# A rebuilt decode-attention-plus-MLP backward kernel: 32x32 vector transposes, tiled TensorE matmuls, weights in slices

## Chip, cores and metric

The kernel runs on one core of one Trainium2 chip. The metric is the device time of one launch in microseconds (us). TensorE is PE in the profile (its weight loads PEld), VectorE is DVE, ScalarE is ACT, GpSimd is POOL and SyncE is SP.

## What is computed

One decode step of two branches that share a layer norm, with all gradients. Inputs and outputs are bf16.

```python
B, Sq, D = 2, 1, 576;  Hq, Hkv, Sk, Dh = 32, 16, 4096, 128;  F = 4608
xn = layernorm(x)
q = (xn @ wq), 32 heads;  k, v = caches [2, 16, 4096, 128], each used by 2 query heads
p = softmax(q k^T * Dh**-0.5);  o = p v;  attn = o @ wo
mlp = ((xn @ w_gate) * (xn @ w_up)) @ w_down
out = x + attn + mlp
returns out and the gradients of x, k_cache, v_cache, wq, wo, w_gate, w_up, w_down for grad_out
```

The caches are 33.5 MB each and their gradients are as large; the five weights are 4.7 to 5.3 MB each, and so are their gradients. The gradients of the caches are outer products: dV[key, :] is the sum over two query heads of p[key] times dO, and dK[key, :] is the sum of dS[key] times q.

## The kernel before

Work comes in three stages, in the order of the code, and a scheduler orders each engine's instructions within what the tile pools allow.

- **Preamble** (lines 111 to 193). Layer norm; wq and wo are loaded whole; wo is transposed on PE (line 173); q and dO for all heads come out transposed, with two columns per weight load.
- **Eight head groups** (loop at lines 233 and 234: 2 batches, 4 groups of G = 4 key-value heads). For each group SP loads four K and four V heads of 1 MB (lines 266 and 272; pools of five buffers each). `scores_pass` (line 217) turns each head by PE: 32 transposes of 128x128 (line 208), eight copies out of PSUM (DVE line 213, ACT line 211) and eight score matmuls of 512 columns (line 225), whose output rows are 8 used rows out of 128, copied to SBUF (line 230). Softmax on rows of 4096 (lines 282 to 292); P and dS are transposed on PE (`rows_T`, line 300) and contracted with V and K, two moving columns per 128x128 weight load (lines 311 and 358). `outer_grad` (line 318) makes dV and dK: 32 matmuls of 512 columns each over 98 rows (line 326), one PSUM bank each, copied to bf16 on ACT for dV (line 336), on ACT and DVE in turn for dK (lines 336 and 334), and stored from POOL in pieces of 256 KB (line 339).
- **Tail** (line 369 on). wo and wq are loaded a second time, then the three MLP weights, each whole; each is transposed on PE where needed (lines 427 and 438); then the five weight gradients are made, copied out and stored in pieces of 64 to 144 KB (lines 559 to 587).

Of the kernel before, what the change touches and what calls it, by code (L numbers as in the profile page):

```python
# [8 lines left out]
AF = mybir.ActivationFunctionType  # L9
ALU = mybir.AluOpType  # L10
# [3 lines left out]
P = 128  # L14


@with_exitstack
def kernel(
# [41 lines left out]
    EPS = 1e-5  # L60

    nfull = D // P
    rem = D - nfull * P
    ND = nfull + (1 if rem else 0)
    DOFF = [c * P for c in range(nfull)] + ([D - P] if rem else [])
    DLO = [0] * nfull + ([P - rem] if rem else [])

    const = ctx.enter_context(tc.tile_pool(name="const", bufs=1))
    ps = ctx.enter_context(tc.tile_pool(name="ps", bufs=2, space=bass.MemoryType.PSUM))

    def ps_tr(shape, dtype=BF16):
# [12 lines left out]

    evac_state = [0]

    def evac(out_ap, in_ap, scale=None, engine=None):
        if engine is None:
            engine = "v" if (evac_state[0] % 2 == 0) else "s"
            evac_state[0] += 1  # L90
        if engine == "v":
            if scale is None:
                nc.vector.tensor_copy(out=out_ap, in_=in_ap)  # L93
            else:
                nc.vector.tensor_scalar(out_ap, in_ap, float(scale), None, op0=ALU.mult)
# [6 lines left out]
    ev_state = [0]

    def ev(out_ap, in_ap):
        if ev_state[0] % 2 == 0:
            nc.vector.tensor_copy(out=out_ap, in_=in_ap)
        else:
            nc.scalar.copy(out_ap, in_ap)
        ev_state[0] += 1

    ident = const.tile([P, P], BF16, name="ident")
    make_identity(nc, ident[:])

    x_bf = const.tile([2, D], BF16, name="x_bf")
    nc.sync.dma_start(x_bf[:], A_x.rearrange("b s d -> (b s) d"))
    x_f = const.tile([2, D], FP32, name="x_f")
    nc.vector.tensor_copy(x_f[:], x_bf[:])
    dy_bf = const.tile([2, D], BF16, name="dy_bf")
    nc.sync.dma_start(dy_bf[:], grad_out.rearrange("b s d -> (b s) d"))
    dy_f = const.tile([2, D], FP32, name="dy_f")  # L120
    nc.vector.tensor_copy(dy_f[:], dy_bf[:])
# [4 lines left out]
    xc = const.tile([2, D], FP32, name="xc")  # L126
    nc.vector.tensor_scalar(xc[:], x_f[:], mu[:], None, op0=ALU.subtract)
    xsq = const.tile([2, D], FP32, name="xsq")
    var = const.tile([2, 1], FP32, name="var")
    nc.vector.tensor_tensor_reduce(  # L130
        out=xsq[:], in0=xc[:], in1=xc[:], scale=1.0 / D, scalar=0.0,
# [7 lines left out]
    xn_f = const.tile([2, D], FP32, name="xn_f")  # L139
    nc.vector.tensor_scalar(xn_f[:], xc[:], rstd[:], None, op0=ALU.mult)  # L140
# [3 lines left out]
    def rows_to_T(rows_bf, name):  # L144
        tp = ps_tr([P, ND, 2], BF16)
        for c in range(ND):
            nc.tensor.transpose(tp[:, c, :], rows_bf[0:2, DOFF[c]:DOFF[c] + P], ident[0:2, 0:2])
        t = const.tile([P, ND, 2], BF16, name=name)
        nc.vector.tensor_copy(t[:], tp[:])
        return t  # L150

    xnT = rows_to_T(xn_bf, "xnT")
    dyT = rows_to_T(dy_bf, "dyT")

    qT_all = const.tile([P, Hq, 2], BF16, name="qT_all")
    doT_all = const.tile([P, Hq, 2], BF16, name="doT_all")
    oT_all = const.tile([P, Hq, 2], BF16, name="oT_all")
    dqT_all = const.tile([P, Hq, 2], BF16, name="dqT_all")

    with tc.tile_pool(name="w1", bufs=1) as w1:  # L160
        wq_sb = w1.tile([P, ND, HD], BF16, name="wq_sb")
        if nfull > 0:
            nc.sync.dma_start(wq_sb[:, 0:nfull, :], A_wq[0:nfull * P, :].rearrange("(c p) n -> p c n", p=P))
        if rem:
            nc.sync.dma_start(wq_sb[:, nfull, :], A_wq[D - P:D, :])
        wo_nat0 = w1.tile([P, Hq, D], BF16, name="wo_nat0")
        nc.sync.dma_start(wo_nat0[:], A_wo.rearrange("(c p) n -> p c n", p=P))
        woT_sb = w1.tile([P, ND, HD], BF16, name="woT_sb")
        for c in range(ND):
            for h8 in range(0, Hq, 8):  # L170
                tp = ps_tr([P, 8, P], BF16)
                for i in range(8):
                    nc.tensor.transpose(tp[:, i, :], wo_nat0[:, h8 + i, DOFF[c]:DOFF[c] + P], ident[:, :])
                ev(woT_sb[:, c, h8 * Dh:(h8 + 8) * Dh], tp[:].rearrange("p i d -> p (i d)"))

        qT_ps = ps_acc([P, Hq, 2])
        for h in range(Hq):
            for c in range(ND):
                lo = DLO[c]
                nc.tensor.matmul(  # L180
                    qT_ps[:, h, :], lhsT=wq_sb[lo:P, c, h * Dh:(h + 1) * Dh],
                    rhs=xnT[lo:P, c, :], start=(c == 0), stop=(c == ND - 1),
                )
        nc.vector.tensor_copy(qT_all[:], qT_ps[:])
        doT_ps = ps_acc([P, Hq, 2])
        for h in range(Hq):
            for c in range(ND):
                lo = DLO[c]
                nc.tensor.matmul(
                    doT_ps[:, h, :], lhsT=woT_sb[lo:P, c, h * Dh:(h + 1) * Dh],  # L190
                    rhs=dyT[lo:P, c, :], start=(c == 0), stop=(c == ND - 1),
                )
        nc.scalar.copy(doT_all[:], doT_ps[:])

    okview = out_2.rearrange("b h (p c) d -> b h p c d", p=P)
    ovview = out_3.rearrange("b h (p c) d -> b h p c d", p=P)
    kview = A_k_cache.rearrange("b h (p c) d -> b h p c d", p=P)
    vview = A_v_cache.rearrange("b h (p c) d -> b h p c d", p=P)

    with tc.tile_pool(name="grp", bufs=1) as gp:  # L200
        GR = 32 * (G - 1) + 2
        tt_state = [0]

        def transposed_tile(src_sb, kt, tagname):
# [417 lines left out]
```

## Time and profile before

| | us |
|---|---|
| median of 2 runs (lowest, highest) | 1140.95 (1140.0, 1141.89) |
| span of the profiled execution | 1133.8 |
| PE, DVE, ACT, POOL busy in it | 861.0, 504.6, 517.7, 287.3 |

The profile comes from one execution, whose own device time is not given apart; its span is taken here, and the median of the runs lies 7.2 us above it. No engine is busy for the whole span, so the average says little: each stage is read for itself.

### The profile page before, as it was taken

The page shows a single profiled execution, that of the slowest core. Times are in us where ns is not written, and L with a number is a line of the kernel's source. Part 1 is how long each engine was busy: PE and PEld are TensorE (multiplying, and loading weights), DVE is VectorE, ACT ScalarE, POOL GpSimd, SP SyncE. Part 2 cuts the span into 40 slices and gives each one's busy share as a digit, 9 for nine tenths or more (in the row PEclk, how much of TensorE's full clock was granted, in tenths as well). Part 3 has the DMA queues.
Part 4 walks back from the last instruction along what each step waited for, and adds up shares of the span by engine and source line. Part 5 has one row for each costly group of instructions (what it writes and reads, how often), then busy time and mean ns, then how long its engine had stood idle before and what let it go on. Part 6 is the DMA issues. An engine that isn't in the chain of part 4 may idle for free. (4 is left out here: it accounts for less than half of the span.)

```text
span 1133.8 us, 20144 instructions
## 1 busy us (share of the span) xinstructions
PE 861.0 (76%) x8208; PEld 511.8 (45%) x8208; DVE 504.6 (45%) x870; ACT 517.7 (46%) x900; POOL 287.3 (25%) x615
## 2 busy tenths in 40 slices
PE   3877788878768877878877878885599497786764
PEld 3755445535445544545553544551279463231210
DVE  1246155346436526615615635533141134774443
ACT  0346556556556555655645646662151230223332
POOL 0100221221131122123023023023000001677775
PEclk9878579678688888867858969975695689656555
DMA  9170760671581483185077057034990500444443
GB/s 345 49 331 3 289 266 39 221 300 74 186 334 76 149 318 128 47 323 226 1 270 288 38 189 294 38 124 190 376 334 26 209 1 33 155 153 141 153 142 123
DMA packets 54429, 197.94 MB, mean 175 GB/s; under 512 B 8472, under 2 KB 21280, under 8 KB 43584
## 3 DMA queue, kind: packets, MB, share of 16 engines
q1 hardware_dynamic: 24768, 104.15, 24.4%
q0 software_dynamic: 29568, 92.50, 21.6%
q8 instruction: 64, 1.05, 0.4%
q14 instruction: 29, 0.24, 0.1%
HBM read 104.14 MB, written 92.48 MB: 173 GB/s over the span
## 5 line engine op out<-in xcount | busy, mean ns | idle before, releaser
L336 ACT CAST dVst<-ps_dkv 128x512 bf16<-128x512 f32 x256 | 142.2, 586 | 120.4 <-PE ps_dkv L326 76.6
L326 PE MATMUL ps_dkv<-doBD,p_sb 98*128 98x512 bf16 x256 | 128.4, 524 | 49.1 <-ACT dVst L336 46.7
L326 PE MATMUL ps_dkv<-qsBD,ds_sb 98*128 98x512 bf16 x256 | 105.5, 462 | 51.0 <-ACT dKst L336 26.8
L334 DVE CAST dKst<-ps_dkv 128x512 bf16<-128x512 f32 x128 | 88.3, 690 | 110.8 <-PE ps_dkv L326 73.7
L339 POOL DMA_DIRECT2D out_dram<-dVst x128 | 68.3, 541 | 259.8 <-ACT dVst L336 259.8
L208 PE MATMUL ps_tr<-ident,V 128*128 128x128 bf16 x1024 | 98.0, 234 | 38.7 <-DVE vT L213 28.0
L208 PEld LDWEIGHTS <-K 128*128 128x128 bf16 x1024 | 83.0, 107 | 79.1 <-issue 43.8
L208 PEld LDWEIGHTS <-V 128*128 128x128 bf16 x1024 | 80.1, 106 | 80.3 <-issue 62.0
L336 ACT CAST dKst<-ps_dkv 128x512 bf16<-128x512 f32 x128 | 75.0, 586 | 86.9 <-PE ps_dkv L326 51.3
L208 PE MATMUL ps_tr<-ident,K 128*128 128x128 bf16 x1024 | 104.9, 237 | 7.3 <-DMA K<-in_A_k_cache_dram 6.0
L339 POOL DMA_DIRECT2D out_dram<-dKst x128 | 68.3, 539 | 148.2 <-ACT dKst L336 70.0
L225 PE MATMUL ps_sc<-kT,qM 128*128 128x512 bf16 x256 | 93.8, 412 | 2.2 <-DVE kT L213 1.0
L213 DVE COPY vT<-ps_tr 128x512 bf16<-128x512 bf16 x171 | 68.1, 422 | 59.9 <-PE ps_sc L225 42.3
L582 PE MATMUL ps_g<-rows,xnP 128*128 128x512 bf16 x130 | 64.5, 565 | 36.7 <-DVE gwq_st L93 11.4
L213 DVE COPY kT<-ps_tr 128x512 bf16<-128x512 bf16 x171 | 68.4, 420 | 48.6 <-PE ps_sc L225 27.5
L225 PE MATMUL ps_sc<-vT,doM 128*128 128x512 bf16 x256 | 89.4, 413 | 0.0
L211 ACT COPY kT<-ps_tr 128x512 bf16<-128x512 bf16 x85 | 50.0, 588 | 37.5 <-PE ps_sc L225 9.7
L211 ACT COPY vT<-ps_tr 128x512 bf16<-128x512 bf16 x85 | 49.7, 585 | 33.0 <-PE ps_sc L225 12.1
L326 PEld LDWEIGHTS <-ds_sb 98*128 98x128 bf16 x256 | 27.7, 109 | 75.2 <-issue 69.0
L568 POOL DMA_DIRECT2D out_dram<-gwo_st x32 | 17.2, 539 | 171.5 <-ACT gwo_st L98 164.7
L300 PEld LDWEIGHTS <-ds_sb 128*128 128x128 bf16 x256 | 31.5, 144 | 58.0 <-issue 57.5
L301 DVE COPY dsT<-ps_tr 128x64 bf16<-128x64 bf16 x32 | 6.1, 192 | 106.0 <-PE ps_tr L300 106.0
(175 smaller groups left out, 1382.7 us busy)
## 6 DMA issues: line engine op xcount, KB each, us to landing
K<-in_A_k_cache_dram SPq DMA_DIRECT2D x32, 1024.0 KB, 9.8
V<-in_A_v_cache_dram SPq DMA_DIRECT2D x32, 1024.0 KB, 6.8
out_dram<-dVst POOLq DMA_DIRECT2D x128, 256.0 KB, 8.0
out_dram<-dKst POOLq DMA_DIRECT2D x128, 256.0 KB, 3.5
wd_sb<-in_B_w_down_dram SPq DMA_DIRECT2D x1, 5184.0 KB
out_dram<-gwd_st POOLq DMA_DIRECT2D x36, 144.0 KB, 2.1
wo_nat<-in_A_wo_dram SPq DMA_DIRECT2D x1, 4608.0 KB, 28.5
wo_sb<-in_A_wo_dram SPq DMA_DIRECT2D x1, 4608.0 KB
```

Source lines behind the costliest of these rows:

```text
L208: nc.tensor.transpose(tp[:, i, :], src_sb[:, c, :], ident[:, :])
L211: nc.scalar.copy(t[:], tp[:])
L213: nc.vector.tensor_copy(t[:], tp[:])
L225: nc.tensor.matmul(s_ps[:], lhsT=masks[l][:].rearrange("p l r -> p (l r)"), rhs=tiles[kt][l][:].rearrange("p c k -> p (c k)"), start=(l == ...
L300: nc.tensor.transpose(tp[:, i, :], src[:, c * P:(c + 1) * P], ident[:, :])
L301: nc.vector.tensor_copy(t[:, 8 * c8:8 * c8 + 8, :].rearrange("p c (l r) -> p c l r", l=G), tp[:, :, :].rearrange("p c (l r) -> p c l r", l ...
L326: nc.tensor.matmul(pk[:, :], lhsT=rows_src[0:GR, c * P:(c + 1) * P], rhs=rhsBD[0:GR, :, :].rearrange("p l d -> p (l d)"), start=True, stop ...
L334: nc.vector.tensor_copy(st[:, :, i, :], pk[:, :].rearrange("p (l d) -> p l d", l=G))
L336: nc.scalar.copy(st[:, :, i, :], pk[:, :].rearrange("p (l d) -> p l d", l=G))
L339: nc.gpsimd.dma_start(oview[b, hkv][:, 8 * c8:8 * c8 + 8, :], st[:, l, :, :])
L568: nc.gpsimd.dma_start(out_ap[j * P:(j + 1) * P, :], st[:])
L582: nc.tensor.matmul(pk[:], lhsT=xnP[:, DOFF[c]:DOFF[c] + P], rhs=rows[:, t * 512:(t + 1) * 512], start=True, stop=True)
```

## The change

The kernel is written anew around one idea: no PE transposes of K and V. A head of K (128 partitions by 4096 bf16) is read as 128x2048 four-byte elements, each a pair of neighbouring bf16, and DVE transposes it in blocks of 32x32 (`t32`). A partition then holds pairs of features, and the score matmul picks the even or the odd one with a moving operand of step two; its weights `W` are block-diagonal and built by POOL (lines 382 and 386), so that all 128 output rows are used: 4 blocks of keys by 8 query heads. A head still takes eight score matmuls of 512 columns, but their result is 128x1024, not 128x4096 (line 414). P and dS are turned by `t32` as well (lines 490 and 511). `contract` has 32 weight columns (rows of P) and 128 moving columns (V or K as loaded), written to four blocks of 32 output partitions in turn; `outer` has 32 rows, in pairs into two PSUM banks, so that one copy takes 1024 columns; one store is 1 MB. The heads of both batches in a group are done one after another (g outside, b inside). Between attentions stands one ninth of the MLP, forward and backward (`mlp_slice`), and wq and wo are loaded by group and once. `evac` gives each copy to DVE or ACT by a running sum. Loads share ten 8 KB buffers ("nat"), stores three ("st"), transposed data two ("X").

```diff
+    def evac(out, in_, cols, bf_in=False):
+        cv = 0.16 + cols * (0.00052 if bf_in else 0.00104)
+        cs = 0.16 + cols * 0.00083
+        if load["v"] + cv < load["s"] + cs:
...
+    def t32(out, in_):
+        nc.vector.transpose(out, in_)
...
+        return sb.tile(list(shape), BF16, tag="nat", bufs=10, name=name)
...
+        return sb.tile(list(shape), BF16, tag="X", bufs=2, name=name)
...
+        return sb.tile(list(shape), BF16, tag="st", bufs=3, name=name)
...
+        def scores(src, Wt):
+            heads = []
+            s_ps = ps_sc()
+            for l in range(G):
+                n = nat([P, NCH, Dh], "kv")
+                nc.sync.dma_start(n[:].rearrange("p c d -> p (c d)"), src[b, G * g + l])
+                heads.append(n)
+                X = xtile([P, NCH * Dh], "X")
+                t32(X[:].bitcast(FP32), n[:].rearrange("p c d -> p (c d)").bitcast(FP32))
+                for half in range(2):
+                    for be in range(4):
+                        nc.tensor.matmul(
+                            s_ps[:, half, :], lhsT=Wt[:, be, l, :],
+                            rhs=view(X[:], 0, P, half * 16 * Dh + 64 * (be // 2) + be % 2, [[Dh, 16], [2, 32]]),
...
+        def contract(rowsT, heads):
+            o_ps = ps_m([P, G, Dh])
+            for l in range(G):
+                for c in range(NCH):
+                    q = c % 4
+                    nc.tensor.matmul(o_ps[32 * q:32 * q + 32, l, :], lhsT=rowsT[:, c, :], rhs=heads[l][:, c, :],
+                                     start=(c < 4), stop=(c >= NCH - 4))
...
+        def outer(r2, bd, oview):
+            for s in range(4):
+                so = stile([P, G, 8, Dh], "so")
+                for k in range(0, 8, 2):
+                    c = 8 * s + k
+                    o = ps_o()
+                    for q in (c % 4, c % 4 + 1):
+                        nc.tensor.matmul(o[:, q % 2, :], lhsT=r2[32 * q:32 * q + 32, c // 4, :],
+                                         rhs=bd[32 * q:32 * q + 32].rearrange("p l d -> p (l d)"), start=True, stop=True)
+                    evac(so[:, :, k:k + 2, :].rearrange("p l c d -> p c l d"),
+                         o[:].rearrange("p c (l d) -> p c l d", l=G), 1024)
+                nc.gpsimd.dma_start(oview[b, :, G * g:G * g + G, 8 * Dh * s:8 * Dh * (s + 1)],
+                                    so[:].rearrange("p l c d -> p l (c d)"))
...
+    for g in range(NGRP):
+        st = group_front(g)
+        for b in range(Bq):
+            attention(st, b)
+            mlp_slice(nslice)
+            nslice += 1
+        group_back(st)
+    while nslice < NFS:
+        mlp_slice(nslice)
+        nslice += 1
```

In `attention` the order of the code is: scores of K, row maximum and softmax, P turned (pT) and its rows (`token_rows`, 32 PE transposes with 32 weight columns, one copy "r"), scores of V, dS (lines 498 to 511), contract(P, V), outer for dV, rows of dS, contract(dS, K), outer for dK.

Three places where the instruction order shows the change.

DVE, softmax of one attention, first before. (s_sb: scores, vT: transposed V copied out of PSUM, pT: transposed P.)

```order
L282 TENSOR_REDUCE mx<-s_sb 128x1
L213 COPY vT<-ps_tr 128x512 x2
L284 TENSOR_SCALAR negb<-mx 128x1
L213 COPY vT<-ps_tr 128x512 x4
L291 RECIPROCAL rs<-rowsum 128x1
L292 TENSOR_SCALAR p_sb<-p_sb,rs 128x4096
L213 COPY vT<-ps_tr 128x512 x13
L301 COPY pT<-ps_tr 128x64
```

The same place now (X: a transposed head, kv: a head as loaded; the X between mx and mr is the second V head).

```order
L467 TENSOR_REDUCE mx<-ps_sc 128x1
L100 STREAM_TRANSPOSE X<-kv 128x2048
L471 COPY mr<-ps_m 1x32
L473 TENSOR_REDUCE m_318<-ps_m 1x32
L474 COPY mr<-m_318 1x128
L478 TENSOR_SCALAR negb<-ps_m 128x1
L486 RECIPROCAL rz<-ps_m 128x1
L488 TENSOR_SCALAR pr<-ex,rz 128x1024
L100 STREAM_TRANSPOSE pT<-pr 128x1024
L100 STREAM_TRANSPOSE X<-kv 128x2048 x2
L498 ISA ds,cs<-pr,ps_sc 128x1024
```

Twenty-odd copies of 512 columns have gone from between the softmax steps; one transpose of a whole head stands inside the chain from maximum to P, and two behind it.

ACT, from the last V scores to the copies of dK, before (dp_sb: scores of V).

```order
L211 COPY vT<-ps_tr 128x512
L230 COPY dp_sb<-ps_sc 128x512 x2
L336 CAST dVst<-ps_dkv 128x4x128 x30
L336 CAST dKst<-ps_dkv 128x4x128
L260 COPY doBD<-ps_tr 128x512
```

The same engine now, from the exponential to the end of the attention (r: rows of P or dS, o_sb: result of a contract, so: dV or dK on its way out).

```order
L481 ACTIVATE ex,z<-ps_sc,negb 128x1024
L91 COPY r_369<-ps_m 128x1024
L91 CAST so<-ps_o 128x2x4x128 x3
L433 COPY o_sb<-ps_m 128x512
L91 CAST so<-ps_o 128x2x4x128 x13
L91 COPY r_672<-ps_m 128x1024
L433 COPY o_sb<-ps_m 128x512
L91 CAST so<-ps_o 128x2x4x128 x9
L398 CAST BD_1147<-ps_m 128x512
```

Copies of scores and of transposed heads are gone from ACT; only three output copies stand ahead of the result of contract(P, V), and thirteen queue behind it.

SP, loads behind the first group, before (DMAHW, PE, DVE with a number: counts that the issue waits for).

```order
L272 DMA V<-in_A_v_cache_dram 128x4096 [waits DMAHW3_49,PE_49]
L266 DMA K<-in_A_k_cache_dram 128x4096 [waits PE_49] x2
L266 DMA K<-in_A_k_cache_dram 128x4096 [waits DMAHW4_49,PE_49]
L266 DMA K<-in_A_k_cache_dram 128x4096 [waits DMAHW5_49,PE_49]
L272 DMA V<-in_A_v_cache_dram 128x4096 [waits DMAHW6_49]
```

The same queue now, behind the first eight heads (wgu: a slice of w_gate and w_up, wd: of w_down).

```order
L236 DMA wgu<-in_B_w_gate_dram 128x4x512 [waits DMAHW1_49,DVE_49,PE_49]
L236 DMA wgu<-in_B_w_up_dram 128x4x512 [waits DMAHW2_49]
L239 DMA wd<-in_B_w_down_dram 128x2304 [waits DMAHW3_49,DVE_49,PE_49]
L407 DMA kv<-in_A_k_cache_dram 128x4096 [waits DMAHW4_49,DVE_49,PE_49]
L407 DMA kv<-in_A_k_cache_dram 128x4096 [waits DMAHW5_49,DVE_49,PE_49]
L407 DMA kv<-in_A_k_cache_dram 128x4096 [waits DMAHW6_49,PE_49]
L407 DMA kv<-in_A_k_cache_dram 128x4096 [waits DMAHW7_49,PE_49]
L407 DMA kv<-in_A_v_cache_dram 128x4096 [waits DMAHW0_49,PE_49]
```

K and V no longer have pools of their own: the slice of the MLP and the next K heads take the buffers that PE frees.

## Rows read from the trace of the kernel before

**Rows 1.** The page, parts 1 and 2: busy time, DMA in 40 slices.

```profile
PE 861.0 (76%) x8208; PEld 511.8 (45%) x8208; DVE 504.6 (45%) x870; ACT 517.7 (46%) x900; POOL 287.3 (25%) x615
DMA  9170760671581483185077057034990500444443
```

**Rows 2.** Busy time by stretch: preamble, eight groups, tail.

```profile
core 0: us, PE busy (x) PEld busy (x) DVE busy (x) ACT busy (x) POOL busy (x), PEclk, DMA share, GB/s
0.00:52.50 52.50, 31.35 (x490) 28.65 (x490) 11.48 (x24) 11.43 (x13) 0.69 (x6) 0.95 0.53 191
52.50:784.50 732.00, 582.76 (x5696) 349.97 (x5696) 350.32 (x614) 412.50 (x708) 155.03 (x380) 0.78 0.48 183
784.50:1133.80 349.30, 246.85 (x2022) 133.17 (x2022) 142.75 (x233) 93.79 (x180) 131.58 (x229) 0.68 0.43 154
```

**Rows 3.** The row maximum's line, one execution per group.

```profile
L282 DVE TENSOR_REDUCE mx<-s_sb x8: 4408/4410/4421, 82.0 to 715.4; 128x1 f32<-128x4096 f32 x8
```

**Rows 4.** Busy time in the last group: scores, contracts with dV, dK alone; then two loads.

```profile
726.00:743.00 17.00, 15.68 (x162) 9.96 (x162) 11.33 (x23) 11.68 (x22) 0.00 (x0) 1.00 0.01 2
747.00:762.00 15.00, 13.63 (x181) 8.35 (x180) 1.21 (x7) 10.69 (x21) 4.26 (x8) 0.73 0.36 142
762.00:784.50 22.50, 17.62 (x33) 3.54 (x31) 10.54 (x16) 10.40 (x18) 8.53 (x16) 0.50 0.47 187
784.50:806.00 21.50, 0.00 (x0) 0.00 (x0) 0.51 (x1) 0.00 (x0) 7.10 (x11) 0.50 0.83 280
806.00:837.00 31.00, 28.60 (x295) 17.58 (x296) 8.63 (x15) 9.54 (x10) 0.00 (x0) 0.90 0.91 334
```

**Rows 5.** Groups of instructions by line and shape: count, busy us, mean ns.

```profile
L336 ACT CAST dVst<-ps_dkv 128x512 bf16<-128x512 f32 x256 | 142.2, 586 | 120.4 <-PE ps_dkv L326 76.6 <-DMA out_dram<-dVst 42.3
L208 PE MATMUL ps_tr<-ident,K 128*128 128x128 bf16 x1024 | 104.9, 237 | 7.3 <-DMA K<-in_A_k_cache_dram 6.0
L334 DVE CAST dKst<-ps_dkv 128x512 bf16<-128x512 f32 x128 | 88.3, 690 | 110.8 <-PE ps_dkv L326 73.7 <-DMA out_dram<-dKst 35.7
L108 ACT COPY woT_sb<-ps_tr 128x1024 bf16<-128x1024 bf16 x10 | 9.8, 1013 | 28.7 <-PE ps_tr L173 28.7
L106 DVE COPY woT_sb<-ps_tr 128x1024 bf16<-128x1024 bf16 x10 | 6.9, 692 | 9.6 <-PE ps_tr L173 9.6
```

**Rows 6.** PE in order of time: start, length, line, count.

```profile
742.86 0.38 PE L326 MATMUL ps_dkv<-doBD,p_sb 98*128 98x512 bf16 x1
743.07 3.08 PE L311 MATMUL ps_acc<-pT,V 128*128 128x2 bf16 x112
759.25 0.59 PE L326 MATMUL ps_dkv<-doBD,p_sb 98*128 98x512 bf16 x2
769.93 1.01 PE L326 MATMUL ps_dkv<-qsBD,ds_sb 98*128 98x512 bf16 x2 [0.35 <-DVE dKst L334]
779.55 0.58 PE L326 MATMUL ps_dkv<-qsBD,ds_sb 98*128 98x512 bf16 x1 [0.36 <-DVE dKst L334]
820.27 7.59 PE L438 MATMUL ps_trw<-ident,wq_nat 128*128 128x128 bf16 x128 [1.06 <-DVE wqT_sb L106]
858.34 3.57 PE L438 MATMUL ps_trw<-ident,wg_sb 128*128 128x128 bf16 x32
```

**Rows 7.** All engines in order of time: softmax of the last group.

```profile
720.36 0.15 DVE L284 TENSOR_SCALAR negb<-mx 128x1 f32<-128x1 f32 x1
720.60 3.71 ACT L287 ACTIVATE p_sb<-s_sb,negb 128x4096 bf16<-128x4096 f32 x1 [3.54 <-DVE negb L284]
```

**Rows 8.** All engines in order of time: the first use of two K heads; the first matmul.

```profile
6.80 0.29 PE L147 MATMUL ps_tr<-ident,xn_bf 2*128 2x2 bf16 x5 [6.80 <-DVE xn_bf L142]
...
59.84 0.61 PE L208 MATMUL ps_tr<-ident,K 128*128 128x128 bf16 x4 [0.76 <-DMA K<-in_A_k_cache_dram]
62.32 0.61 PE L208 MATMUL ps_tr<-ident,K 128*128 128x128 bf16 x4 [0.77 <-DMA K<-in_A_k_cache_dram]
```

**Rows 9.** The page, part 3: bytes read and written.

```profile
HBM read 104.14 MB, written 92.48 MB: 173 GB/s over the span
```

More of the change, by code (lines that the diff above doesn't have):

```diff
@@ L102 @@
[L102 to L109, printed above, removed]
+    NB = D // 64
+    DOFF = [0, 128, 256, 384, 448]
+    FS = 512
+    NFS = F // FS
+    FC = FS // P
+    HB = D // 2
+    const = ctx.enter_context(tc.tile_pool(name="const", bufs=1))
+    sb = ctx.enter_context(tc.tile_pool(name="sb", bufs=1))
+    ps = ctx.enter_context(tc.tile_pool(name="ps", bufs=1, space=bass.MemoryType.PSUM))
@@ L138 @@
     nc.vector.reciprocal(rstd[:], rstd[:])
-    xn_f = const.tile([2, D], FP32, name="xn_f")
-    nc.vector.tensor_scalar(xn_f[:], xc[:], rstd[:], None, op0=ALU.mult)
+    nc.vector.tensor_scalar(xn_f[:], xn_f[:], rstd[:], None, op0=ALU.mult)
     xn_bf = const.tile([2, D], BF16, name="xn_bf")
     nc.vector.tensor_copy(xn_bf[:], xn_f[:])
[L144 to L179, printed above, removed]
@@ new lines @@
+    xnT = const.tile([P, 5, 2], BF16, name="xnT")
+    tp = ps_m([P, 5, 2], BF16)
+    for c in range(4):
+        nc.tensor.transpose(tp[:, c, :], xn_bf[0:2, c * P:(c + 1) * P], ident[0:2, 0:2])
+    nc.tensor.transpose(tp[0:64, 4, :], xn_bf[0:2, 512:576], ident[0:2, 0:2])
+    nc.vector.tensor_copy(xnT[:, 0:4, :], tp[:, 0:4, :])
+    nc.vector.tensor_copy(xnT[0:64, 4, :], tp[0:64, 4, :])
+    Wdy = const.tile([P, NB, 2, P], BF16, name="Wdy")
+    nc.gpsimd.memset(Wdy[:], 0.0)
+    dyr = ps_m([P, NB, 2, 2])
@@ new lines @@
+    dyp = sb.tile([2, 4, NB, 2, 32], BF16, tag="X", bufs=2, name="dyp")
+    for a in range(4):
+        nc.vector.tensor_copy(
+            view(dyp[:], 0, 2, 32 * a, [[256, NB], [128, 2], [1, 32]]),
+            view(dy_bf[:], 0, 2, 0, [[64, NB], [1, 2], [2, 32]]),
+        )
+    for k in range(NB):
+        for e in range(2):
+            nc.tensor.matmul(
+                dyr[:, k, e, :], lhsT=view(dyp[:], 0, 2, (2 * k + e) * P, [[1, P]]),
+                rhs=ident[0:2, 0:2], start=True, stop=True,
+            )
@@ new lines, in mlp_slice @@
+        nc.vector.tensor_add(acc[:], acc[:], yd[:])
+        dve(1.5)
+        rp = ps_m([2, 2, 512], BF16)
+        rows = sb.tile([2, 3, FS], BF16, tag="rows", bufs=1, name="rows")
+        for c in range(FC):
+            nc.tensor.transpose(rp[:, 0, c * P:(c + 1) * P], hT[:, 0, c, :], ident[:])
+        nc.vector.tensor_copy(rows[:, 0, :], rp[:, 0, :])
+        rp = ps_m([2, 2, FC, P], BF16)
+        for w in range(2):
+            for c in range(FC):
+                nc.tensor.transpose(rp[:, w, c, :], hT[:, 1 + w, c, :], ident[:])
@@ new lines, in mlp_slice @@
+        nc.vector.tensor_copy(
+            rows[:, 1:3, :].rearrange("b w (p c) -> b w c p", c=FC), rp[:],
+        )
+        dve(1.5)
+        std = stile([P, FC * D], "std")
+        outer_flat(std, rows[:, 0, :], 0, FC)
+        nc.gpsimd.dma_start(out_8[f0:f0 + FS, :].rearrange("(p c) n -> p (c n)", c=FC), std[:])
+        stt = sb.tile([64, 2, FS], BF16, tag="stt", bufs=2, name="stt")
+        ot = ps_o()
+        for w in range(2):
+            nc.tensor.matmul(ot[0:64, w, :], lhsT=xn_bf[0:2, 512:576], rhs=rows[0:2, 1 + w, :], start=True, stop=True)
@@ new lines, in mlp_slice @@
+        evac(stt[:], ot[0:64], 1024)
+        for w, out in enumerate((out_6, out_7)):
+            stw = stile([P, 4, FS], "stw")
+            for dc in range(0, 4, 2):
+                o = ps_o()
+                for k in range(2):
+                    nc.tensor.matmul(o[:, k, :], lhsT=xn_bf[0:2, (dc + k) * P:(dc + k + 1) * P],
+                                     rhs=rows[0:2, 1 + w, :], start=True, stop=True)
+                evac(stw[:, dc:dc + 2, :], o[:], 1024)
+            nc.gpsimd.dma_start(out[0:512, f0:f0 + FS].rearrange("(c p) n -> p c n", p=P), stw[:])
+            nc.gpsimd.dma_start(out[512:576, f0:f0 + FS], stt[:, w])
@@ L487 @@
-    nc.vector.tensor_copy(o0_bf[:], o0_f[:])
-    nc.sync.dma_start(out_0.rearrange("b s d -> (b s) d"), o0_bf[:])
-    pa = ps_sc()
-    pb = ps_sc()
-    for j in range(NF):
-        for (vt_, wt_) in ((dgT_bf, wgT_sb), (duT_bf, wuT_sb)):
-            first = (j == 0 and vt_ is dgT_bf)
-            last = (j == NF - 1 and vt_ is duT_bf)
-            nc.tensor.matmul(pa[0:2, 0:NB0], lhsT=vt_[:, j, :], rhs=wt_[:, j, 0:NB0],
-                             start=first, stop=last)
-            nc.tensor.matmul(pb[0:2, 0:NB1], lhsT=vt_[:, j, :], rhs=wt_[:, j, NB0:D],
-                             start=first, stop=last)
@@ new lines, in group_front @@
+        dof = sb.tile([P, GH, 32], FP32, tag="dof", bufs=1, name="dof")
+        t32(dof[:].rearrange("p c n -> p (c n)"), do_ps[:])
+        nc.vector.tensor_copy(qd[:, 1], dof[:, :, 0:2])
+        dve(1.0)
+        rp = ps_m([P, 2, 4, GH * 2])
+        for t in range(2):
+            for be in range(4):
+                nc.tensor.matmul(
+                    rp[:, t, be, :],
+                    lhsT=sel[:, be].rearrange("p a i -> p (a i)"),
+                    rhs=qd[:, t].rearrange("p h b -> p (h b)"), start=True, stop=True,
+                )
```

716 lines of the change are left out of this document (326 added, 390 removed).

## Prediction

> **What bounds the kernel now.** I read the page's busy times first, then busy time by stretch, then the last group in small stretches, then prices by line. No engine is the bound: PE is busy for 76% of the span, DVE and ACT for 45%, and the DMA line jumps between 0 and 9 [rows 1]. By stretch the span is 52.5 us of preamble, 732 us of eight groups and 349 us of tail [rows 2]; one group lasts (715.4 - 82.0) / 7 = 90.5 us [rows 3]. Inside the last group the reader is to see the bound move: while heads are turned and scored PE is busy for 15.7 of 17 us at full clock and DMA stands still; in contract and dV PE still has 13.6 of 15 us; in dK alone PE is at clock 0.50 and waits for copies, and DMA gets to 0.47 [rows 4]. So the stages load PE, ACT and DMA one after another. In the tail PE waits for a whole weight (21.5 us with nothing on PE), then works while DMA idles. What is to gain is PE work in the groups, and a tail that could lie beside the groups.
>
> **What the change removes.** The 2048 PE transposes of K and V and their copies: K alone shows 1024 transposes with 104.9 us of PE time [rows 5]. The second load of wq and wo, so reads fall from 104.14 MB to 92.5 MB (33.5 MB for each cache, 25.4 MB of weights); writes stay 92.48 MB [rows 9]. The tail as a stage: its work stands between attentions.
>
> **Prices.** PE: 512 columns cost 0.59 - 0.38 = 0.21 us at full and 1.01 - 0.58 = 0.43 at half clock; a fresh 128x128 weight with 128 columns 7.59 / 128 = 0.059 at full and 3.57 / 32 = 0.11 at half; with two columns 3.08 / 112 = 0.027 [rows 6]. A first matmul alone takes 0.38, 0.17 beyond its columns. ACT: 0.59 for 512 and 1.01 for 1024 columns; DVE: 0.69 for 512 columns from PSUM in f32 and for 1024 in bf16 [rows 5], 4.41 for 4096 [rows 3], which makes 0.158 + 0.00104 per column: 1.22 for 1024. From one engine to the next 0.09 us (720.51 to 720.60) [rows 7].
>
> Three things are not in this trace. First, the transposes on DVE. One head is 128x2048 four-byte elements: at DVE's f32 rate 0.158 + 2.13 = 2.28 us. Below, bf16 speed (0.53 us per 1024 above the fixed part) gives 1.2; above, each bf16 counted alone, as 4096 elements, gives 4.41. I take 2.28, the rate of every f32 row on DVE. Per attention three heads lie openly in the chain and part of four more, so 4.41 adds about 10 us per attention (83 in all), 1.2 saves 3 (25). Second, matmuls with 32 weight columns or 32 rows. Per contract matmul the ends are 0.027 (one quarter of the 128 columns, by four beside each other, is the same 0.027 at half clock) and 0.11; per pair in outer 0.21 (both at once, full clock) and 0.86 (in turn, half clock). I take 0.059 and 0.43, what dense work in order costs at full clock. Third, a moving operand of step two: 0.21 to 0.86 (read twice, half clock); I take the plain price. The upper end would add some 10 us per attention.
>
> On the second, the rows say nothing of tiles, only that PE runs at full clock where it is dense and at 0.50 in dK [rows 4]. [...]
>
> **The sum for one attention with its slice**, from the last K score on:
> 1. Maximum to P turned. Maximum 1.22, a whole V head on DVE 2.28 (it is queued ahead of the next short step), three short copies 0.45, bias 0.15, exponential about 1.2 (1.01 for the copy, some more for the sum), reciprocal 0.15, scaling 1.22, transpose 1.22, three lone matmuls 0.5, ten hand-overs 0.9: 9.3 us.
> 2. V scores to dS's row sum. Two heads 4.56, the last head's eight matmuls 3.4 (half clock after idling), the sum 1.22, hand-overs 0.3: 9.5 us.
> 3. contract(P, V). PE does all 128 in a row before it returns to dV: 128 x 0.059 = 7.6 us. ACT's fourth output copy is queued behind o_sb and waits here, with dV's stores behind it. The rest of dS is covered.
> 4. Rows of dS 32 x 0.059 = 1.9, contract(dS, K) 7.6, eleven output pairs between them 4.7: 14.2 us on PE. ACT's eleven copies (11.2) lie beside it.
> 5. The last sixteen output pairs: ACT 13 x 1.02, one "r" 1.02, two block-diagonals 1.2, hand-overs 1.6: 17.0 us; three copies on DVE and PE's 16 x 0.43 plus about 108 small ones at 0.059 (13.3) beside it.
> 6. End of the slice and the next K scores on PE: 40 transposes 2.4, 40 two-column matmuls 1.1, outputs 3.1, 32 scores 6.7, hand-overs: 14 us; ACT's 7.7 beside it. The next heads' transposes on DVE run here.
>
> Steps 1 to 5 are 57.6 us; eight of them 461, seven of step 6 98. Between groups come eight more copies on ACT (8.4), dO's 18 matmuls (2), masks on POOL, and K scores that can no longer hide (6.7): 20 us, three times 60. Start: the first matmul comes at 6.8 us, as before; K heads land 2.48 us apart [rows 8], so wq, wo and four heads (6.3 MB) are there by about 19 us; dO, masks and 32 half-clock scores end at 31. End: slice, group, last slice, final sums: 8 + 9 + 13 + 10 and hand-overs, 45.
>
> **DMA.** From step 3 to 6 (53 us) eight heads or slices (7.8 MB) and 9.8 MB of stores are asked for. At 334 / 0.91 = 367 GB/s [rows 4] that is 48 us, so it fits barely. The wgu load waits for contract(P, V) on PE, and wd and all next K and V loads are queued behind it on SP; if they come late, DVE waits for a head, and the chain with it. I allow 3 us per attention, 24 in all. Before, a preamble without stores and a tail with late weights hid this.
>
> Sum: 461 + 98 + 60 + 31 + 45 + 24 = 719 us of span, plus the 7.2 that lie between the span and the median of the runs: 726 us. As floors, ACT has some 380 us of copies now and DVE some 355, 64 heads x 2.28 = 146 of it; both stay under the sum.
>
> **Rivals.**
> - Tiles don't run beside each other, and PE stays at half clock with 32-row and 32-column work. For it: dK's stretch at 0.50 [rows 4], since PE there has pauses, as it will in steps 4 and 5. Against: dense stretches were at 1.00. Step 3 becomes 14.1, step 4 160 x 0.11 + 11 x 0.86 = 27.1, step 5 about 20.2: 22.6 more per attention, 907 us.
> - DMA alone bounds, all else hides. 185 MB / 367 GB/s = 504 us; with a start, an end and a share of 0.85 about 590. For it: the share was 0.91 where loads alone ran. Against: steps 1 and 2 (19 us) have little to move, since buffers come free only in steps 3 to 6.
> - Slower than before: the DVE transpose pays its fixed 0.158 us for each block of 32 columns: 64 x (0.158 + 0.033) = 12.2 us a head. DVE is in order, so steps 1, 2 and 6 and the turns of P and dS stretch; about 63 us of span per extra us a head, 726 + 63 x 9.9 = 1350. It decides from 9.1 us a head on. Against: no DVE row costs over 1.04 ns per element beyond a fixed part.
> - That the change doesn't do what it says: the order has no PE transpose of K or V left, so this falls away.
>
> **Chances.** Forecast 0.72, tiles 0.14, DMA 0.11, transposes 0.03. The range goes from 726 - 25 - 50 (contract at 0.027, ACT bounding step 4) - 24 = about 620 up to 890, most of the way to the tile rival or to 4.41 us a head with part of it; the rest, some 0.2, is left out. A measurement of this kernel can tell about 2% from no change. The time stays below that bound in all but the last rival and a tile rival with every matmul at half clock: faster 0.95, same 0.02, slower 0.03.
>
> **What would show it.** Step 1: the transpose of a 128x2048 head near 2.28 us, and mr waiting behind it. Steps 3 and 4: 128 contract matmuls in 7 to 8 us, ACT's o_sb waiting for PE. Step 5: ACT nearly full with copies of 1.02. DMA: heads that DVE waits for little. The tail: no stretch of PE idling for a weight, about 15 us after the last attention for each slice. The forecast is wrong if one attention takes under 60 or over 95 us, if contract's matmuls cost 0.1 us or more, if a head costs over 4 us on DVE, or if DVE waits mostly for loads.

## Result and the profile after

The changed kernel takes 884.59 us (median of two, 883.98 to 885.2) against 1140.95: a ratio of 0.777, 95% interval 0.771 to 0.782. That lies in the range, but 159 us above the 726 that were forecast; the profiled execution's span is 883.4 us, against a sum of 719.

The page's busy times, the granted clock and DMA in 40 slices, and the bytes; they answer to [rows 1] and [rows 9]:

```profile
PE 692.2 (78%) x6469; PEld 338.6 (38%) x6469; DVE 390.3 (44%) x439; ACT 364.7 (41%) x395; POOL 110.1 (12%) x211
PEclk9885559555685557755579555855558555775555
DMA  9459623993309850896315972399430985084322
HBM read 92.48 MB, written 92.48 MB: 209 GB/s over the span
```

The reader is to see the many 5s in the clock line. The mean granted clock is 0.62 of full speed; TensorE did 1739 matmuls fewer than before, and yet was busy for 692 of 883 us.

The line of the row maximum (it answers to [rows 3], one execution per attention now):

```profile
L467 DVE TENSOR_REDUCE mx<-ps_sc x8: 1185/1205/1225, 33.1 to 755.2; 128x1 f32<-128x1024 f32 x8
```

One attention with its slice takes (755.2 - 33.1) / 7 = 103 us: 91.5 us on the mean of the four with no group boundary behind them, 118.7 of the three with one. Now busy time by stretch, the six steps of the prediction for the fifth attention, and after them step 6 of the sixth, which holds a group boundary (it answers to [rows 2, 4]):

```profile
core 0: us, PE busy (x) PEld busy (x) DVE busy (x) ACT busy (x) POOL busy (x), PEclk, DMA share, GB/s
453.99:463.03 9.04, 3.76 (x11) 1.85 (x12) 6.21 (x10) 1.21 (x2) 0.73 (x4) 0.66 0.00 1
463.03:471.92 8.89, 7.76 (x65) 3.07 (x64) 5.85 (x4) 2.94 (x4) 0.82 (x4) 0.96 0.01 2
471.92:476.44 4.52, 4.00 (x150) 3.27 (x153) 2.69 (x5) 2.75 (x5) 0.00 (x0) 1.00 0.40 123
476.44:497.26 20.82, 10.91 (x194) 6.39 (x189) 1.55 (x2) 12.50 (x15) 3.02 (x4) 0.68 1.02 400
497.26:517.06 19.80, 16.35 (x128) 8.22 (x128) 7.40 (x11) 12.85 (x14) 2.26 (x3) 0.50 0.89 340
517.06:545.30 28.24, 28.21 (x130) 10.17 (x130) 15.80 (x10) 8.69 (x9) 3.96 (x6) 0.50 0.48 169
...
606.72:664.00 57.28, 50.38 (x326) 24.31 (x326) 26.96 (x26) 17.86 (x19) 8.75 (x22) 0.55 0.44 157
```

Steps 1 and 2 are as forecast (9.3 and 9.5). Step 3 is shorter (7.6), step 4 longer (14.2), and step 6 twice as long (14): TensorE is busy for 28.21 of 28.24 us there, at half clock. The step with a group boundary was to take 34 us.

Lines by shape (they answer to [rows 5]):

```profile
L100 DVE STREAM_TRANSPOSE X<-kv 128x2048 f32<-128x2048 f32 x64 | 146.8, 2303 | 51.2 <-PE ps_sc L414 51.0
L91 ACT CAST so<-ps_o 128x1024 bf16<-128x1024 f32 x221 | 215.9, 1020 | 148.3 <-PE ps_o L458 92.5
L430 PE MATMUL ps_m<-kv,pT 128*32 128x128 bf16 x1024 | 15.8, 219 | 0.0
```

A head is turned on DVE in 2.30 us (2.28 was taken). PE in order of time (it answers to [rows 6]): the scores' and dV's prices at full clock, the contraction, a long wait in step 4, and scores between two-row products in step 6:

```profile
468.76 1.90 PE L414 MATMUL ps_sc<-X,W 128*128 128x512 bf16 x8 [0.18 <-DVE X L100]
470.59 0.39 PE L458 MATMUL ps_o<-BD,r 32*128 32x512 bf16 x3
472.69 1.97 PE L430 MATMUL ps_m<-kv,pT 128*32 128x128 bf16 x128
483.82 0.39 PE L458 MATMUL ps_o<-BD,r 32*128 32x512 bf16 x2 [0.20 <-ACT so L91]
484.14 0.61 PE L430 MATMUL ps_m<-kv,dsT 128*32 128x128 bf16 x14
491.14 0.61 PE L458 MATMUL ps_o<-BD,r 32*128 32x512 bf16 x2 [6.39 <-ACT so L91]
536.22 1.03 PE L315 MATMUL ps_o<-rows,xn_bf 2*128 2x512 bf16 x2
537.18 1.89 PE L414 MATMUL ps_sc<-X,W 128*128 128x512 bf16 x4
```

Eight score matmuls take 1.90 us at full clock, four take 1.89 in step 6. All 128 contraction matmuls take 1.97 us, 15 ns each, where 128 with a whole 128x128 weight took 7.59 [rows 6], and a pair of dV's matmuls takes 0.39 us, where one alone took 0.38 [rows 6]: both kinds run beside each other. At 484 us TensorE waits 6.39 us for a copy, and ScalarE's own row says why that copy came late; the second row is the sum over the span, from the view of waits:

```profile
490.08 3.76 ACT L91 CAST so<-ps_o 128x1024 bf16<-128x1024 f32 x4 [6.31 <-DMA out_dram<-so]
...
ACT so L91 <- DMA out_dram<-so: 51.1, 17, 6.3
```

All three store buffers were on their way out. So two theories stand: A, the clock stays at half where it was priced as full; C, store buffers are missing in step 4.

### The profile page after: what moved, and what is told of

Its sections match the earlier page's. It is cut to its first block, busy times and chain, and to the rows that moved or that the text cites. A ratio compares the mean times of both kernels' runs of the same rounds, so it can differ in the third digit from the quotient of the medians.

```text
span 883.4 us, 14680 instructions
## 1 busy us (share of the span) xinstructions
PE 692.2 (78%) x6469; PEld 338.6 (38%) x6469; DVE 390.3 (44%) x439; ACT 364.7 (41%) x395; POOL 110.1 (12%) x211
## 3 DMA queue, kind: packets, MB, share of 16 engines
q1 hardware_dynamic: 28064, 92.49, 28.1%
q0 software_dynamic: 24240, 92.48, 27.5%
HBM read 92.48 MB, written 92.48 MB: 209 GB/s over the span
## 5 line engine op out<-in xcount | busy, mean ns | idle before, releaser
L91 ACT CAST so<-ps_o 128x1024 bf16<-128x1024 f32 x221 | 215.9, 1020 | 148.3 <-PE ps_o L458 92.5
L458 PE MATMUL ps_o<-BD,r 32*128 32x512 bf16 x512 | 130.9, 531 | 83.6 <-ACT so L91 49.4
L414 PE MATMUL ps_sc<-X,W 128*128 128x512 bf16 x512 | 170.8, 488 | 15.0 <-POOL W L382 9.7
L100 DVE STREAM_TRANSPOSE X<-kv 128x2048 f32<-128x2048 f32 x64 | 146.8, 2303 | 51.2 <-PE ps_sc L414 51.0
L462 POOL DMA_DIRECT2D out_dram<-so x64 | 48.4, 756 | 409.5 <-ACT so L91 377.4
L414 PEld LDWEIGHTS <-W 128*128 128x128 bf16 x512 | 56.3, 117 | 111.9 <-issue 74.3
L88 DVE CAST so<-ps_o 128x1024 bf16<-128x1024 f32 x35 | 43.0, 1229 | 27.2 <-PE ps_o L458 17.9
L226 PE MATMUL ps_o<-ident,wgu 128*128 128x128 bf16 x288 | 44.2, 308 | 5.8 <-DVE so L88 4.7
L430 PE MATMUL ps_m<-kv,dsT 128*32 128x128 bf16 x1024 | 38.9, 267 | 0.9 <-issue 0.9
L315 PE MATMUL ps_o<-rows,xn_bf 2*128 2x512 bf16 x72 | 36.5, 614 | 1.0 <-DVE stw L88 0.8
L430 PEld LDWEIGHTS <-dsT 128*32 128x32 bf16 x1024 | 21.5, 111 | 25.8 <-issue 25.8
L100 DVE STREAM_TRANSPOSE Xd<-wd 128x1152 f32<-128x1152 f32 x9 | 12.4, 1377 | 39.9 <-DMA wd<-in_B_w_down_dram 39.9
## 6 DMA issues: line engine op xcount, KB each, us to landing
kv<-in_A_k_cache_dram SPq DMA_DIRECT2D x32, 1024.0 KB, 14.2
```

What stands on the lines that cost most here:

```text
L88: nc.vector.tensor_copy(out=out, in_=in_)
L91: nc.scalar.copy(out, in_)
L100: nc.vector.transpose(out, in_)
L226: nc.tensor.transpose(tp[:, k - k0, dc * P:(dc + 1) * P], src(k, dc), ident[:])
L315: nc.tensor.matmul(o[:, k, :], lhsT=xn_bf[0:2, (dc + k) * P:(dc + k + 1) * P], rhs=rows[0:2, 1 + w, :], start=True, stop=True)
L414: nc.tensor.matmul(s_ps[:, half, :], lhsT=Wt[:, be, l, :], rhs=view(X[:], 0, P, half * 16 * Dh + 64 * (be // 2) + be % 2, [[Dh, 16], [2, 3 ...
```

## Experiments

Each run stands beside a run of the kernel before on the same chip (1139.37 to 1141.18 us). The table has the means over the eight attentions of steps 4 and 5, of the four steps 6 without and the three with a group boundary, and the stretch from the last dK matmul to the end, read by the same bounds in each trace. e1 to e8 were executed once each, e9 and e10 four times; e9's four times span 6.8 us, so a difference of that size between two rows says little.

| run | us | step 4 | step 5 | step 6 | with boundary | end |
|---|---|---|---|---|---|---|
| forecast | 726 | 14.2 | 17.0 | 14 | 34 | 45 |
| changed kernel | 884.6 | 19.6 | 19.9 | 27.9 | 57.2 | 67.5 |
| e1_pad | 834.7 | 19.5 | 19.9 | 21.3 | 50.0 | 61.8 |
| e2_fill | 917.1 | 20.2 | 23.9 | 28.1 | 56.3 | 66.7 |
| e3_pad_fill | 870.9 | 20.6 | 23.9 | 21.5 | 48.8 | 58.9 |
| e4_st4 | 841.1 | 14.8 | 19.7 | 28.2 | 56.4 | 67.6 |
| e5_rows128 | 877.2 | 20.5 | 19.7 | 26.4 | 55.0 | 67.2 |
| e6_pad_rows128 | 826.6 | 20.6 | 19.8 | 20.5 | 48.2 | 57.8 |
| e7_pad_st4 | 797.6 | 15.3 | 19.8 | 22.3 | 49.4 | 61.3 |
| e8_all | 788.8 | 15.0 | 20.2 | 20.9 | 48.6 | 57.2 |
| e9_vgate | 780.9 | 15.0 | 18.9 | 21.0 | 49.3 | 55.7 |
| e10_split | 787.8 | 11.2 | 26.5 | 18.6 | 45.3 | 56.5 |

**Rows or pauses (e1, e2, e3).** Is it the two-row products that go with the half clock, or the pauses of steps 4 and 5? e1 pads the two rows with zero rows in tiles that are cleared once; e2 adds one matmul over 128 rows ahead of each output pair, whose result the pair overwrites.

```diff
...
-            nc.tensor.matmul(ot[0:64, w, :], lhsT=xn_bf[0:2, 512:576], rhs=rows[0:2, 1 + w, :], start=True, stop=True)
+            nc.tensor.matmul(ot[0:64, w, :], lhsT=xnP[:, 512:576], rhs=rows[:, 1 + w, :], start=True, stop=True)
...
```

```diff
+                    for _ in range(1):
+                        nc.tensor.matmul(o[:, 0, :], lhsT=ident[:], rhs=bd[:].rearrange("p l d -> p (l d)"),
+                                         start=True, stop=True)
                     for q in (c % 4, c % 4 + 1):
...
```

> The edit: the outer products of the slices and of the group's end, which contract over 2 rows, contract over 128 rows of which 126 are zero; the number of matmuls and of columns stays. Theory A (the granted clock stays at 0.50 after steps 4 and 5 because the matmuls of the stretch use few rows of the array): the clock of step 6 rises from 0.50 to 0.8 or more, the step shortens from 28 to about 18 us, the group boundary from 57 to about 40, and the whole from 884 to about 780. Rival B (it stays low because of the pauses of steps 4 and 5 and of the two-column matmuls, not because of the rows): clock 0.50 to 0.55 in step 6, and 884 within 10. In both, steps 1 to 4 stay as they are.

> The edit: ahead of each pair of output matmuls one further matmul of 128 rows by 128 columns of weights with 512 moving columns writes the buffer that the pair then overwrites; it adds 32 x 8 x 2... that is 256 matmuls in all, 16 for each of the 16 outputs of an attention. Theory A (the clock falls in steps 4 and 5 because TensorE does little there): the clock of steps 4 and 5 rises from 0.68 and 0.50 to 0.8 or more, step 5 takes 16 us instead of 20, step 6 about 20 instead of 28, the whole about 800. Rival B (the clock does not depend on this): each added matmul costs its 0.43 us at half clock, 7 us in step 5 and a part of that in step 4, and the whole comes to 920 to 940.

> Both edits together: outer products over 128 padded rows, and a further matmul of 512 columns ahead of each output pair. If theory A holds in both its parts (few rows, and little work), TensorE stays at full clock from step 1 to the end of step 6, which then takes 16 us, and the whole 720 to 760. If only one part matters, the time is that of the better of the two runs within 10. If the clock is set by neither, 920 to 940.

Busy time by stretch, steps 5 and 6 of the fifth attention, in e1 and then in e2:

```profile
472.31:492.08 19.77, 16.32 (x128) 8.20 (x128) 7.40 (x11) 12.88 (x14) 2.26 (x3) 0.50 0.87 333
492.08:512.74 20.66, 18.90 (x131) 9.54 (x130) 15.38 (x10) 8.68 (x9) 3.95 (x6) 0.79 0.66 231
```

```profile
511.22:535.14 23.92, 23.11 (x139) 8.91 (x138) 7.30 (x11) 11.63 (x12) 2.26 (x3) 0.50 0.82 310
535.14:564.57 29.43, 29.39 (x137) 10.89 (x136) 15.80 (x11) 9.18 (x10) 3.95 (x6) 0.50 0.39 138
```

e1 is 50 us faster with the same matmuls and columns: after the same step 5 at 0.50, step 6 has 0.79 and TensorE's time falls from 28.2 to 18.9 us. (0.79 is a mean: the clock is 0.50 for the first 8.5 us of the step and 1.00 for the rest.) So it matters that these products stand on few rows; whether the number of rows does it, or something else that goes with the padding, no run tells apart. e2 takes the pauses away (23.11 of 23.92 us busy in step 5) and leaves the few-row products in; the clock stays at 0.50, and the added columns cost 33 us, a little under what rival B counted: the pauses alone are not the cause. e3 came out at neither end: it has e1's step 6 and e2's step 5, so the filler only costs. The 780 forecast for e1 was too low: the clock rose, but step 6 still takes 21.3 us and the group boundary 50.

**Store buffers (e4).**

```diff
-        return sb.tile(list(shape), BF16, tag="st", bufs=3, name=name)
+        return sb.tile(list(shape), BF16, tag="st", bufs=4, name=name)
...
```

> The edit: four store buffers instead of three; their room comes from the second buffer of three small tiles (the weight slice's tail, the store tile of its last 64 rows, and the block of dS times K). Theory C (steps 4 and 5 are late because ScalarE waits for a store buffer): ScalarE's 51 us of waiting for stores falls to under 20, step 4 shortens from 20 to 16 us, and the whole to about 850. Rival D (the DMA engines are full there, 400 GB/s, and buffers only move the wait): step 4 shortens by at most 2 us and step 5 grows by as much; 884 within 10.

Step 4 of the fifth attention, and the wait, in e4:

```profile
453.80:468.22 14.42, 10.90 (x194) 6.35 (x189) 1.55 (x3) 13.28 (x15) 3.01 (x4) 0.77 1.03 411
...
ACT so L91 <- DMA out_dram<-so: 13.7, 11, 1.9
```

Theory C holds in step 4: the wait falls from 51.1 to 13.7 us, the step from 19.6 to 14.8, and nothing is given back in step 5: 8 x 4.8 = 39 of the 43 us. ScalarE, which was to lie beside TensorE in step 4, is now nearly full itself (13.28 of 14.42 us), with TensorE busy for 10.90; the DMA engines are full as well (1.03).

**The output pairs on 128 rows (e5, e6).** The block products stand four times, zero outside their own 32 rows.

```diff
-            nc.scalar.copy(bd[:], bp[:])
...
+            for q in range(4):
+                nc.scalar.copy(bd[32 * q:32 * q + 32, q], bp[32 * q:32 * q + 32])
...
-                        nc.tensor.matmul(o[:, q % 2, :], lhsT=r2[32 * q:32 * q + 32, c // 4, :],
-                                         rhs=bd[32 * q:32 * q + 32].rearrange("p l d -> p (l d)"), start=True, stop=True)
+                        nc.tensor.matmul(o[:, q % 2, :], lhsT=r2[:, c // 4, :],
+                                         rhs=bd[:, q].rearrange("p l d -> p (l d)"), start=True, stop=True)
```

> The edit: the output matmuls of steps 4 and 5 contract over all 128 rows: the block products stand four times in a tile that is zero outside the 32 rows of their own block, and the turned rows are taken whole; the number of matmuls and of columns stays. Theory A (few rows hold the clock at half): the clock of step 5 rises from 0.50 to 0.9 or more, its TensorE time falls from 16.3 to about 8 us and the step to 17, then held by the stores; step 6 starts at full clock and shortens from 28 to 20 to 24; the whole 820 to 840. Rival B (the pauses between the pairs hold it): clock 0.50 to 0.55 in step 5, and 884 to 895, the three further ScalarE copies of each block product included.

> The edit: no outer product over 2 or 32 rows is left, all contract over 128 rows with zeros. Theory A: TensorE keeps 0.9 or more of its clock through steps 5 and 6; step 6 takes 17 us (padded outer products of the slices alone: 21), the group boundary 42 (there 50), step 5 17 (there 20), and the whole about 765. Rival B (the rows of the output matmuls do not matter): 835 within 10, as with the slices' outer products padded alone.

Steps 5 and 6 of the fifth attention in e6, and step 6 of the sixth, with its boundary:

```profile
470.21:488.68 18.47, 15.19 (x121) 8.66 (x122) 8.92 (x13) 9.73 (x11) 2.26 (x3) 0.79 0.87 335
488.68:508.34 19.66, 16.18 (x132) 8.74 (x133) 15.48 (x11) 12.24 (x16) 3.95 (x6) 1.00 0.64 226
...
571.74:621.43 49.69, 40.89 (x323) 22.50 (x324) 25.89 (x25) 20.85 (x25) 8.78 (x22) 0.74 0.49 175
```

In e5 the clock of step 5 rises to 0.67 to 0.83, but the step keeps its 19.7 us: there the clock is not what ends last. Where the two-row products stand unpadded the clock falls back (0.54 to 0.73 in step 6). In e6 the fifth's step 6 runs at 1.00 and takes 19.7 us, not 17, with TensorE busy for 16.18. Both totals missed theory A's numbers: step 5 gave nothing, and step 6 and the boundary gave less than was forecast. For step 5 two pairs in e5, at half and at full clock, show one reason:

```profile
84.40 1.05 PE L463 MATMUL ps_o<-BDm,r 128*128 128x512 bf16 x2
85.88 0.59 PE L463 MATMUL ps_o<-BDm,r 128*128 128x512 bf16 x2
```

On 128 rows the two matmuls of a pair no longer run beside each other: the pair takes 1.05 us at half clock and 0.59 at full, where it took 0.61 and 0.39 on 32 rows. For the pairs the padding that brought the clock up took the gain back.

**All together, and step 5 (e7 to e10).** e7 joins e1 and e4, e8 all three edits.

> The edit: the slices' and the group's outer products padded to 128 rows and four store buffers (room from the tails and from the input's second copy). If the two losses lie in different steps they add up: 884 less 50 less 43, that is 790 within 8. If the DMA engines are the next bound, the second gain is smaller: 805 to 830, with a DMA share near 1.0 that reaches into step 6.

> The edit: all three: 128 rows in every outer product, and four store buffers. If clock and store buffers were the whole of the shortfall, step 4 takes 14 us, step 5 17, step 6 17, the group boundary 42, and the whole 715 to 735, near the 726 that was forecast. If the DMA engines bound it from there, steps 4 and 5 keep 15 and 20 us at a DMA share of 1.0 and 400 GB/s and the whole stays at 745 to 770.

e7's 797.6 is the sum of both gains, within the 8 us allowed: the two losses are separate. e8's 788.8 fits neither branch: steps 4 and 5 take 15 and 20 us with a DMA share of 1.0 in both, as the second branch has them, but the whole lies above its 770, since step 6 and the boundary stay above 17 and 42. e9 therefore takes the loads out of step 5:

```diff
...
+                if gate is not None:
+                    nc.vector.tensor_copy(n[0:1, 0, 0:2], gate[0:1, 0:2])
                 nc.sync.dma_start(n[:].rearrange("p c d -> p (c d)"), src[b, G * g + l])
...
```

> The edit, on top of the run with all three: the loads of the next V heads wait until the first K head of the same attention has been turned (a copy of two elements into each V buffer reads that result), so that they no longer run beside the output stores of step 5 but in the end of step 6 and in step 1, where the DMA engines stood idle. Rival D (loads and stores together fill the DMA engines in step 5, 8 MB at 420 GB/s are 20 us): step 5 shortens from 20 to 10 to 14 us, its DMA share falls below 0.9, and the whole from 789 to 720 to 745. If the stores alone take the 20 us, or the waits at TensorE and the evictions do: step 5 stays at 19 to 22, and the whole at 785 or above; if the V heads then come late, step 2 grows from 9.5 to 12 or more.

Step 5 of the fifth attention in e8 and in e9:

```profile
444.20:464.64 20.44, 16.07 (x121) 9.09 (x122) 8.83 (x13) 9.69 (x11) 2.26 (x3) 0.73 1.02 421
```

```profile
437.80:456.43 18.63, 15.73 (x123) 8.60 (x122) 9.16 (x13) 10.21 (x11) 2.26 (x3) 0.77 0.80 318
```

The share falls to 0.80, but the step shortens from 20.4 to 18.6 us only, by 1.3 us on the mean of the eight (before a group boundary the share stays at 1.02): theory D falls as the main bound of step 5, which would have left 10 to 14 us. e9 is the fastest version: 780.86 us (776.55 to 783.31), 0.685 of the kernel before, interval 0.681 to 0.689. In e9's step 5 TensorE waits for copies, in order of time:

```profile
88.48 0.59 PE L479 MATMUL ps_o<-BDm,r 128*128 128x512 bf16 x2 [0.23 <-DVE so L88]
89.62 1.87 PE L479 MATMUL ps_o<-BDm,r 128*128 128x512 bf16 x4 [0.54 <-DVE so L88]
```

e10 copies each output buffer in two halves:

```diff
-                    evac(so[:, :, k:k + 2, :].rearrange("p l c d -> p c l d"),
-                         o[:].rearrange("p c (l d) -> p c l d", l=G), 1024)
+                    nc.scalar.copy(so[:, :, k, :], o[:, 0, :].rearrange("p (l d) -> p l d", l=G))
+                    nc.vector.tensor_copy(out=so[:, :, k + 1, :], in_=o[:, 1, :].rearrange("p (l d) -> p l d", l=G))
...
```

> The edit, on top of the run with the gated V loads: each output buffer (1024 columns) is copied out in two halves, the first by ScalarE, the second by VectorE, side by side, instead of whole by the one or the other. Theory E (step 5 is held by the loop through the two output buffers: pair of matmuls 0.6 us, copy 1.0 to 1.2, two hand-overs of 0.09, so 1.9 us a round, two buffers, 0.95 us a pair, 15 us for sixteen pairs): a round becomes 0.6 + 0.7 + 0.2 = 1.5 us, the pairs take 12 us, step 5 shortens from 18.6 to 14 to 16 us and the whole from 781 to 750 to 765. Rival F (the slice's matmuls between the pairs, or the store's own rate, set step 5): step 5 stays at 17.5 to 20 and the whole at 775 to 790; VectorE's added copies may then make step 6 longer.

It takes 787.78 us (ratio 0.692, 0.689 to 0.695). Step 5 takes 26.5 us, outside the numbers of both theories, and step 4 11.2. As an experiment it does not tell E and F apart, because the halves did not run side by side; the view of waits of e10:

```profile
DVE so L482 <- ACT so L481: 72.3, 118, 1.6
```

Late in the step pairs came 1.0 us apart, which is 0.59 + 0.59 + 0.69 and hand-overs for two buffers, as E's loop reckons it for halves in turn. Higher clock, more buffers and fewer loads were each tried, and none shortened step 5 by more than 1.3 us. The trace of e9 says why no single one did: its fifth step 5 in two parts, and a wait from each.

```profile
437.80:445.46 7.66, 7.66 (x85) 5.74 (x84) 0.81 (x4) 3.41 (x4) 0.46 (x1) 0.56 1.01 414
445.46:456.43 10.97, 8.07 (x44) 2.86 (x41) 8.35 (x10) 6.80 (x8) 1.80 (x3) 0.93 0.65 251
...
442.10 1.01 ACT L91 CAST so<-ps_o 128x1024 bf16<-128x1024 f32 x1 [2.84 <-PE ps_o L479]
...
452.51 0.38 PE L406 MATMUL ps_m<-ident,dM 128*128 128x128 bf16 x4 [1.05 <-DVE rowsP L308]
```

In the first part TensorE is busy without a pause, with the slice's matmuls between the pairs and the clock at 0.56, and ScalarE waits for it: rival F. In the second eleven pairs come some 1.0 us apart and TensorE waits for copies, by theory E, and once for VectorE's copy of the slice's rows (2.41 us). This is read from one trace; what step 5 would take with either part mended no run shows.

## Why the prediction was right and where it was wrong

That it is faster by far came as forecast: PE matmuls fell from 8208 to 6469, reads from 104.14 to 92.48 MB. The stretches tell where the time was gained: the preamble falls from 52.5 to 33.1 us and the tail from 349.3 [rows 2] to 67.5, while the stretch of the eight groups grows from 732 to 782.8 us, now with more than seven of the nine slices in it. So the gain is the work of the tail, taken in by groups that grew by 51 us; what the missing PE transposes gave toward that no run shows alone.

By the prediction's own sign (an attention of over 95 us) the forecast is missed, with 103. That 884.6 still lies under 890 is luck: that end was set for matmuls in turn or for dearer transposes, and neither came. Of the 164 us by which the span is longer than the sum:

- **Step 6 failed, and with it the boundary and the end** (+125 us on the seven steps between attentions, +22.5 at the end). "14 us" was worked with full-clock prices, because dense stretches had been at 1.00 [rows 4]. Here TensorE was dense (28.21 of 28.24 us in the fifth) and the clock 0.50; with the products on 128 rows (e6) it was 1.00 in the third and fifth, 0.84 in the first and seventh. Full rows give back 66 of these 148 us (e6's columns against the changed kernel's: 4 x 7.4 + 3 x 9.0 + 9.7). The rest of step 6 is size: at clock 1.00 it has 16.2 us of PE work, where 13.3 were counted, and 3.5 us of waits. The boundary takes 48, where 34 were counted, and the end 58, where 45 were, both in e6 still at clocks of 0.74 to 0.79: how much of that is size and how much clock is open.
- **Step 4 was mis-sized** (+43): a wait for a free store buffer was no term. With a fourth buffer 14.8 stands against 14.2, but by another way: TensorE, which was to set the step, is busy for 10.90 us, since contractions and pairs cost less than was taken, and ScalarE for 13.28, where 11.2 were counted. The 3 us per attention set aside for loads (24 in all) were not needed in that form: DVE does not wait for a K or V head. It waits for w_down (39.9 us in eight waits), in step 4, where ScalarE and the stores set the time.
- **Step 5** (+23): ScalarE was not nearly full (12.85 of 19.80 us). TensorE is the bound of the step's first 7.7 us, busy throughout at clock 0.50, as it was in e9 at 0.56; behind that the pairs and their copies wait for each other.
- **Step 3 was too long** (-25): a contraction matmul costs 15 ns here, under the lower bound of 27, which was a quarter of a half-clock matmul; the stretch ran at full clock. The contraction is 1.97 of the 4.52 us; the copy behind it and the small matmuls were no term.
- Steps 1 and 2, the transposes on DVE and the moving operand of step two came out as taken: 2.30 us a head (that every f32 row on DVE has the rate behind 2.28, and none a higher one, the trace before does not show: over 576 columns line 127 takes 0.507 us and line 522 1.175), 0.22 us for a strided score matmul at full clock ((1.90 - 0.17) / 8, without what the last takes beyond its columns); the start took 33.1 us instead of 31.

The rival "tiles in turn, at half clock" was right in its second half alone, and there not for step 3, which ran at 1.00: 907 and 884.6 are near each other by another way, since tiles do run beside each other (15 ns a contraction matmul, 0.39 us a pair) and step 6, which that rival left at 14 us, took the time. The slower rival ended with the 2.30 us a head, and DMA alone was no bound: its share is 0.00 and 0.01 in steps 1 and 2, as was held against it. Where contraction matmuls and pairs alternate, in step 4, rounds of some 15 matmuls and a pair come 0.92 us apart, and TensorE waits 0.20 us of each for ScalarE, whose copies set the pace (nine in 8.58 us). What the alternation itself costs beside them is not shown.

## What to carry to other kernels

Read the granted clock beside the busy time of the same stretch before a matmul price is taken over: a stretch that was 100% busy here (28.21 of 28.24 us) ran at 0.50. Outer products over few rows went with it; padding those over two rows with zeros cost no column and gave 50 us, while padding the pairs over 32 rows ended their running side by side (0.59 us a pair at full clock, against 0.39) and gave step 5 nothing. When loads and stores start in the same step, count store buffers as a term of their own: ScalarE waited 51.1 us for three here, 13.7 for four.

## What the runs showed of the hardware

TensorE's clock stayed at 0.50 while it was busy for 28.21 of 28.24 us (the fifth step 6) and for 23.11 of 23.92 us (the fifth step 5 in e2), and was 0.79 (a mean of 0.50 and 1.00) and 1.00 in the fifth step 6 of e1 and e6, where zero rows had been added to the same columns. By the busy time of the records the stretch at the higher clock was the less busy one here (16.18 of 19.66 us in e6). Matmuls of 32 weight columns and 128 moving columns, written to four blocks of output partitions in turn, came 15 ns apart (1.97 us for 128). Two output matmuls over 32 rows each took 0.39 us together at full clock, and 0.59 over 128 rows (e5). 512 columns of a moving operand of step two took 0.22 us, plain ones 0.21 [rows 6].
